# Norm sums of later batches eight steps sooner, k's inverse norms over SyncE's queue, logits further behind the sums: a kernel of channel attention and SwiGLU

## The chip, the cores and the metric

One core of a Trainium2 chip. The metric is the time of one execution in device microseconds (us); lower is better. A run also reports its span (first to last instruction); the time is 1.7 to 1.9 us longer in every run with the row on GpSimd, and 1.9 to 2.6 us longer in every run with it on SyncE, so spans of the two kinds can't be compared as times. Engines: PE (matmuls), PEld (weight loads), DVE (VectorE), ACT (ScalarE), POOL (GpSimd), SP (SyncE, which issues transfers).

## The reference, cut to what matters

```python
B, N, C = (4, 6016, 256)              # q, k, v; then d_ff = 1536
qn = q / (norm(q, axis=1) + 1e-6);  kn = k / (norm(k, axis=1) + 1e-6)
s = kn.transpose(0, 2, 1) @ qn / tau                # 256 x 256 for each batch
a = softmax(s)
x = v @ a
out = (silu(x @ w_gate) * (x @ w_val)) @ w_out      # 24064 x 256
```

The kernel folds `a` into both weights of each batch: `x @ w_gate = v @ (a @ w_gate)`. So a batch needs its softmax before its own large matmuls start, and this preparation is done in the background of the batch before it.

## The kernel before

The loop goes over 48 chunks of 512 (or 384) rows, 12 steps each. Every step has four matmuls for g and v, a silu on ScalarE, a product on VectorE, and two matmuls of the previous chunk's output. In each step a plan of background work may add something for the next batch.

```python
for f in range(FH):                                  # 12 steps of a chunk
    g_ps, v_ps, mv = gv_matmuls(b, ci, f)            # PE, PSUM buffers: 2 for g, 2 for v
    silu = gv_silu(g_ps, mv)                         # ScalarE
    gv_product(f, sv, silu, v_ps, mv)                # VectorE
    prev.step()                                      # PE, output of the previous chunk
    background(b + 1, ci * FH + f)
    # ... v loads (GpSimd's queue), v transposes (SyncE's queue), output copies and stores
```

The background of one batch, in order: loads of q and k, 24 pairs of squares with their sums on GpSimd (`norm_acc`), a split into three bf16 parts, column sums on PE, inverse norms on GpSimd. Those of k lie one to a partition; logits need them along a row. So they go out to DRAM as a row and come back spread over all partitions:

```python
def norm_cols(b):
    # ... column sums on PE, copy on VectorE, two powers on GpSimd -> inv [128, 4]
    row = dram.tile([C], FP32, tag="ink_row")
    nc.gpsimd.dma_start(out=row.rearrange("(h p) -> p h", p=P), in_=inv[:, CH:])
    ink = work.tile([P, C], FP32, tag="ink")
    nc.gpsimd.dma_start(out=ink, in_=row.partition_broadcast(P))

def logits(b, jh):                                   # VectorE waits here for ink
    nc.vector.scalar_tensor_tensor(out=state[b, "s"][:, jh, :], in0=kq[:, jh, :],
        scalar=inv[:, jh:jh + 1], in1=ink, op0=ALU.mult, op1=ALU.mult)
# then: tanh (ScalarE), four reciprocals (VectorE), exponentials (VectorE),
# row sums (PE), twelve weight products (PE)
```

The plan, the same for each later batch (144 steps):

```python
SQ0 = 21;  S1 = SQ0 + (5 * NP) // 2 + 1              # NP = 24, so S1 = 82
plan[S1].append((norm_split,))
plan[S1 + 10].append((norm_cols,))                   # with row and spread in it
plan[S1 + 24].append((logits, 0));  plan[S1 + 25].append((logits, 1))
plan[S1 + 26].append((half_tanh,))
# reciprocals S1+29..32, exponentials S1+33, row sums S1+35, weights from S1+36
```

## Time and profile before

| | |
|---|---|
| median of 3 runs at first, of 4 with the later ones | 812.73 us, 813.04 us (812.66 to 813.95) |
| profiled run | 811.27 us, span 809.5 us |
| PE busy | 98% |
| one step in the steady part | 1.295 us = 6 matmuls, 0.216 us apart |

A line of the page's groups reads: line, engine, operation, tiles, number; busy us, mean ns of one; idle time just before them and what ended it. The prediction shows the lines that matter. The page lists 3,905 PE matmuls and 3,979 weight loads. A second profile of the same kernel (the first experiment) has all the 3,979 matmuls, and its rows of the three large groups end so:

```profile
L439 PE MATMUL g_ps<-vT,Wg 128*128 128x512 bf16 (+1 forms) x1128 | 330.7, 375 | 0.0
L439 PE MATMUL v_ps<-vT,Wv 128*128 128x512 bf16 (+1 forms) x1128 | 330.4, 374 | 0.0
L480 PE MATMUL o_new<-sv,w_out_sb 128*128 128x512 bf16 (+1 forms) x1104 | 324.5, 376 | 0.0
```

The 1.2 to 1.3 us of idle time ahead of each group in the first profile were matmuls without a record, not waits: with all records there the idle time is 0.0.

### The profile page before, as it was taken

The numbers are of one execution on the slowest core, as the hardware profiler recorded it, in microseconds if no ns is written. First come the engines' busy times: TensorE is split into PE (matmuls) and PEld (weight loads), VectorE is DVE, ScalarE is ACT, GpSimd is POOL, SyncE is SP. The second block draws the span as 40 slices with busy tenths as digits, with TensorE's granted clock in tenths as the row PEclk, the third lists the DMA queues.
The fourth block names the chain that finished last, engine by engine and source line by source line (L and its number), as shares of the span: only waits on it lengthen the run. The fifth ranks groups of instructions, "written<-read, shape, count | busy, mean of one in ns | idle before, by whom it ended". The sixth has DMA issues, their size and how long they took to land.

```text
span 809.5 us, 11903 instructions
## 1 busy us (share of the span) xinstructions
PE 790.1 (98%) x3905; PEld 385.5 (48%) x3979; DVE 550.1 (68%) x841; ACT 455.6 (56%) x803; POOL 260.9 (32%) x320
## 2 busy tenths in 40 slices
PE   4999999999999999999999999999999999999998
PEld 2644444444454444444454444444445444444446
DVE  4777887658666778766766787866766665665654
ACT  4566666555555666555555666655555555555553
POOL 4415888431011787722010377742100000000000
PEclk9999999999999999999999999999999999999999
DMA  9995999659798899566889799763866656565533
GB/s 90 144 153 106 146 181 170 127 92 163 126 171 141 173 156 159 151 131 73 162 153 146 157 164 181 128 138 80 185 131 143 137 130 131 144 130 129 117 113 98
DMA packets 201070, 112.34 MB, mean 139 GB/s; under 512 B 149088, under 2 KB 187744, under 8 KB 200256
## 3 DMA queue, kind: packets, MB, share of 16 engines
q1 hardware_dynamic: 182720, 84.11, 44.0%
q0 software_dynamic: 18144, 27.41, 31.6%
q8 instruction: 31, 0.51, 0.3%
q14 instruction: 31, 0.25, 0.1%
q10 hardware_dynamic: 144, 0.07, 0.0%
HBM read 79.04 MB, written 60.43 MB: 172 GB/s over the span
## 4 chain that ended last, share of the span: by engine, by line
PE 95%; DMA 3%; issue 1%; ACT 0%; DVE 0%; POOL 0%; ACTq 0%; POOLq 0%
PE g_ps L439 30%; PE v_ps L439 30%; PE o_new L480 29%; PE ps L408 2%; DMA q_sb<-in_q_dram 2%; PE kq_new L168 2%; PE o_new L533 1%; DMA k_sb<-in_k_dram 1%; ACT silu L445 0%; PE last_ps L557 0%; DVE sv L449 0%; PE ss_new L195 0%; PE kq_new L173 0%; PE ps L398 0%; PE unit_ps L408 0%
## 5 line engine op out<-in xcount | busy, mean ns | idle before, releaser
L449 DVE TENSOR_TENSOR sv<-silu,v_ps 128x512 bf16<-128x512 bf16 (+1 forms) x576 | 387.3, 673 | 224.7 <-ACT silu L445 223.5
L445 ACT ACTIVATE silu<-g_ps 128x512 bf16<-128x512 f32 (+1 forms) x576 | 339.1, 589 | 292.9 <-PE g_ps L439 245.1
L439 PE MATMUL v_ps<-vT,Wv 128*128 128x512 bf16 (+1 forms) x1109 | 326.3, 374 | 1.2
L439 PE MATMUL g_ps<-vT,Wg 128*128 128x512 bf16 (+1 forms) x1105 | 325.8, 375 | 1.3
L480 PE MATMUL o_new<-sv,w_out_sb 128*128 128x512 bf16 (+1 forms) x1078 | 318.9, 375 | 1.2
L439 PEld LDWEIGHTS <-Wv 128*128 128x128 bf16 x1152 | 112.7, 98 | 131.0 <-issue 0.6
L300 POOL TENSOR_TENSOR acc_new<-acc_new,sq 128x512 f32<-128x512 f32 x135 | 156.1, 1156 | 56.0 <-DVE sq L290 41.9
L480 PEld LDWEIGHTS <-w_out_sb 128*128 128x128 bf16 x1104 | 108.0, 98 | 126.3
L439 PEld LDWEIGHTS <-Wg 128*128 128x128 bf16 x1152 | 109.6, 98 | 122.2
L126 POOL DMA_DIRECT2D vb_new<-in_v_dram x47 | 24.2, 516 | 265.5 <-DMA vT<-vb_new 264.6
L490 DVE COPY pl<-o_new 128x512 uint16<-128x512 uint16 (+1 forms) x92 | 62.3, 677 | 9.5 <-ACT pl L489 9.5
L290 DVE TENSOR_TENSOR sq<-q_sb 128x512 bf16<-128x512 fp8e5 x72 | 66.5, 924 | 0.0
L489 ACT COPY pl<-o_new 128x512 uint16<-128x512 uint16 (+1 forms) x92 | 53.2, 578 | 19.3 <-PE o_new L480 17.2
L291 ACT ACTIVATE sq<-k_sb 128x512 bf16<-128x512 fp8e5 x72 | 44.2, 615 | 0.0
L168 PE MATMUL kq_new<-k_sb,q_sb 128*128 128x512 fp8e5 x184 | 35.6, 319 | 0.9 <-DMA q_sb<-in_q_dram 0.9
L111 POOL DMA_DIRECT2D q_sb<-in_q_dram x45 | 25.2, 561 | 14.4 <-DMA k_sb<-in_k_dram 9.9
L168 PEld LDWEIGHTS <-q_sb 128*128 128x256 fp8e5 x184 | 22.9, 140 | 9.4 <-DMA q_sb<-in_q_dram 2.0
L195 PE MATMUL ss_new<-sq,ones_bf 128*128 128x256 bf16 x83 | 14.7, 334 | 11.1 <-ACT sq L185 11.1
L111 POOL DMA_DIRECT2D k_sb<-in_k_dram x42 | 22.9, 549 | 1.2 <-POOLq L741 0.8
L295 POOL TENSOR_TENSOR acc_new<-sq 128x512 f32<-128x512 bf16 x3 | 3.5, 1153 | 49.2 <-DVE sq L290 49.2
L195 PEld LDWEIGHTS <-ones_bf 128*128 128x128 bf16 x83 | 9.3, 117 | 15.1 <-issue 10.9
L408 PEld LDWEIGHTS <-exT 128*128 128x128 bf16 x104 | 10.0, 98 | 10.9 <-DMA w_gate_sb<-in_moe_w_gate_dram 0.2
(98 smaller groups left out, 209.0 us busy)
## 6 DMA issues: line engine op xcount, KB each, us to landing
rows<-pl SPq DMA_DIRECT2D x86, 256.0 KB, 3.1
out_dram<-ot_new SPq DMA_DIRECT2D x43, 512.0 KB, 4.0
vb_new<-in_v_dram POOLq DMA_DIRECT2D x43, 256.0 KB, 4.5
q_sb<-in_q_dram POOLq DMA_DIRECT2D x36, 128.0 KB, 6.4
k_sb<-in_k_dram POOLq DMA_DIRECT2D x33, 128.0 KB, 7.1
ot_new<-rows SPq DMA_TRANSPOSE x92, 3.7
k_sb<-in_k_dram POOLq DMA_DIRECT2D x5, 256.0 KB, 9.0
rows<-pl SPq DMA_DIRECT2D x6, 192.0 KB, 2.4
```

The costliest lines, as they stand in the source:

```text
L111: nc.gpsimd.dma_start(out=dst[:, gs:gs + gm, :], in_=src[b].rearrange("(p s) c -> p s c", s=NS)[:, gs:gs + gm, :])
L168: nc.tensor.matmul(kq[:, jh, :], q_sb[:, ps:ps + 2, js], k_sb[:, ps:ps + 2, :], start=(t == 0 and jh == 0), stop=last, perf_mode=DR, skip_ ...
L290: nc.vector.tensor_mul(sq[:, :pm, 0, :], q_sb[:, ps:ps + pm, :], q_sb[:, ps:ps + pm, :])
L291: nc.scalar.activation(sq[:, :pm, 1, :], k_sb[:, ps:ps + pm, :], ACT.Square)
L300: nc.gpsimd.tensor_tensor(out=acc, in0=acc, in1=sq[:, s, :, :], op=ALU.add)
L408: nc.tensor.matmul(ps, state[b, "exT"][:, jh, ih * P:(ih + 1) * P], (w_gate_sb, w_val_sb)[w][:, jh, cols], start=(jh == 0), stop=(jh == CH ...
L439: nc.tensor.matmul(dst[:, :mv], W[:, kk, fs], vT[:, kk, :mv], start=(kk == 0), stop=(kk == CH - 1))
L445: nc.scalar.activation(silu[:, :mv], g_ps[:, :mv], ACT.Silu)
L449: nc.vector.tensor_mul(sv[:, f, :mv], silu[:, :mv], v_ps[:, :mv])
L480: nc.tensor.matmul(self.o_ps[h][:, :self.mv], w_out_sb[:, f, h * P:(h + 1) * P], self.sv[:, f, :self.mv], start=(f == 0), stop=(f == FH - 1))
L489: nc.scalar.copy(pl[:, 0, :self.mv], halves[:, 0, :self.mv])
L490: nc.vector.tensor_copy(pl[:, 1, :self.mv], halves[:, 1, :self.mv])
```

## The change

Its intent, as far as the code tells: take the round trip of the row out of GpSimd's queue, where the loads behind it stood still, and give the preparation more room ahead of its use. The diff, cut:

```diff
+    def norm_row(b):
         row = dram.tile([C], FP32, tag="ink_row")
-        nc.gpsimd.dma_start(out=row.rearrange("(h p) -> p h", p=P), in_=inv[:, CH:])
+        nc.sync.dma_start(out=row.rearrange("(h p) -> p h", p=P),
+                          in_=state[b, "inv"][:, CH:])
+    def norm_spread(b):
         ink = work.tile([P, C], FP32, tag="ink")
-        nc.gpsimd.dma_start(out=ink, in_=row.partition_broadcast(P))
+        nc.sync.dma_start(out=ink, in_=state[b, "row"].partition_broadcast(P))
@@ plan
-            step = 7 + 11 * (g - half_g)             # half_g = 6; batches 2 and 3
+            step = 9 + 5 * g if b == 1 else 7 + 10 * (g - 7)
-    SQ0 = 21
+        SQ0 = 21 if b == 1 else 13
-    plan[S1 + 10].append((norm_cols,))
-    plan[S1 + 24].append((logits, 0))
+        plan[S1 + 8].append((norm_cols,))
+        plan[S1 + 13].append((norm_row,))
+        plan[S1 + 18].append((norm_spread,))
+        S2 = S1 + (26 if b == 1 else 30)
+        plan[S2].append((logits, 0))
 ...     # tanh, reciprocals, exponentials, row sums, weights follow S2 as they followed S1 + 24
```

From column sums to logits there were 14 steps; now there are 18 in batch 1 and 22 in batches 2 and 3. Logits stand at step 108 in batch 1 and 104 in the others, for 106 before.

More of the change, by code (lines that the diff above doesn't have):

```diff
@@ L331, in norm_cols @@
         state[b, "inv"] = inv
+    def norm_row(b):
         row = dram.tile([C], FP32, tag="ink_row")
-        nc.gpsimd.dma_start(out=row.rearrange("(h p) -> p h", p=P), in_=inv[:, CH:])
+        nc.sync.dma_start(out=row.rearrange("(h p) -> p h", p=P),
+                          in_=state[b, "inv"][:, CH:])
+        state[b, "row"] = row
+    def norm_spread(b):
         ink = work.tile([P, C], FP32, tag="ink")
-        nc.gpsimd.dma_start(out=ink, in_=row.partition_broadcast(P))
+        nc.sync.dma_start(out=ink, in_=state[b, "row"].partition_broadcast(P))
         state[b, "ink"] = ink
@@ L566, in finish @@
                     nc.sync.dma_start(out=self.dst[:, j, cols], in_=last_sb)
-    LOAD0, SQ0 = 9, 21
-    plan = [[] for _ in range(STEPS)]
-    first_loads = [[] for _ in range(STEPS)]
-    early_loads = [[] for _ in range(STEPS)]
-    late_loads = [[] for _ in range(STEPS)]
-    half_g = len(groups) // 2
-    for g in range(len(groups)):
-        for which in range(2):
-            first_loads[LOAD0 + 5 * g].append((load_qk, g, which))
-            step = 7 + 11 * (g - half_g)
-            if step < 0:
-                early_loads[step + STEPS].append((load_qk, g, which))
-            else:
-                late_loads[step].append((load_qk, g, which))
@@ L584 @@
-    for t in range(NP):
-        step = SQ0 + (5 * t) // 2
-        plan[step].append((norm_acc, t))
-        if t % 2 == 1:
-            plan[step + 1].append((gemm1_pair, t - 1))
-            plan[step + 1].append((gemm1_pair, t))
-    S1 = SQ0 + (5 * NP) // 2 + 1
-    plan[S1].append((norm_split,))
-    plan[S1 + 10].append((norm_cols,))
-    plan[S1 + 24].append((logits, 0))
-    plan[S1 + 25].append((logits, 1))
-    plan[S1 + 26].append((half_tanh,))
-    for n in range(4):
-        plan[S1 + 29 + n].append((recip, n))
@@ L598, with make_plan @@
-    plan[S1 + 33].append((exponentials,))
-    plan[S1 + 35].append((row_sums,))
-    for u in range(len(wp_units)):
-        plan[S1 + 36 + (u * 3) // 2].append((wp_unit, u))
+    def make_plan(b):
+        plan = [[] for _ in range(STEPS)]
+        early = [[] for _ in range(STEPS)]
+        for g in range(len(groups)):
+            step = 9 + 5 * g if b == 1 else 7 + 10 * (g - 7)
+            at = plan[step] if step >= 0 else early[step + STEPS]
+            at.append((load_qk, g, 0))
+            at.append((load_qk, g, 1))
+        SQ0 = 21 if b == 1 else 13
+        for t in range(NP):
+            step = SQ0 + (5 * t) // 2
+            plan[step].append((norm_acc, t))
+            if t % 2 == 1:
+                plan[step + 1].append((gemm1_pair, t - 1))
+                plan[step + 1].append((gemm1_pair, t))
+        S1 = SQ0 + (5 * NP) // 2 + 1
+        plan[S1].append((norm_split,))
+        plan[S1 + 8].append((norm_cols,))
[3 more added lines that the diff above has]
+        plan[S2].append((logits, 0))
+        plan[S2 + 1].append((logits, 1))
+        plan[S2 + 2].append((half_tanh,))
+        for n in range(4):
+            plan[S2 + 5 + n].append((recip, n))
+        plan[S2 + 9].append((exponentials,))
+        plan[S2 + 11].append((row_sums,))
+        for u in range(len(wp_units)):
+            plan[S2 + 12 + (u * 3) // 2].append((wp_unit, u))
+        return plan, early
@@ L603, in background @@
+    plans = {b: make_plan(b) for b in range(1, B)}
     def background(b, step):
-        loads = first_loads if b == 1 else late_loads
-        for what, *args in loads[step] + plan[step]:
+        for what, *args in plans[b][0][step]:
             what(b, *args)
         if b + 1 < B:
-            for what, *args in early_loads[step]:
+            for what, *args in plans[b + 1][1][step]:
                 what(b + 1, *args)
```

## The prediction

> **What bounds the kernel now.** I read the page first: the busy shares, the 40 slices, and the chain that ended last.
>
> ```profile
> span 809.5 us, 11903 instructions
> PE 790.1 (98%) x3905; PEld 385.5 (48%) x3979; DVE 550.1 (68%) x841; ACT 455.6 (56%) x803; POOL 260.9 (32%) x320
> PE   4999999999999999999999999999999999999998
> PEclk9999999999999999999999999999999999999999
> PE 95%; DMA 3%; issue 1%; ACT 0%; DVE 0%; POOL 0%; ACTq 0%; POOLq 0%
> ```
>
> PE is 9 tenths or more busy in 38 of 40 slices at the full granted clock; the chain is PE for 95% and a DMA for 3% (the opening loads, 7.1 + 19.1 = 26 us in the chain, which this change leaves alone). But PE's ends are modelled, so "busy" could hide waits. The second reading is therefore the groups of PE with the idle time just before them, the third the spacing of the matmuls.
>
> ```profile
> L439 PE MATMUL v_ps<-vT,Wv 128*128 128x512 bf16 (+1 forms) x1109 | 326.3, 374 | 1.2
> L439 PE MATMUL g_ps<-vT,Wg 128*128 128x512 bf16 (+1 forms) x1105 | 325.8, 375 | 1.3
> L480 PE MATMUL o_new<-sv,w_out_sb 128*128 128x512 bf16 (+1 forms) x1078 | 318.9, 375 | 1.2
> ```
>
> The last number of each row is all the idle time ahead of some 1,100 matmuls: 1.2 + 1.3 + 1.2 = 3.7 us together. The timeline of VectorE gives the beat, since it makes one product per step:
>
> ```profile
> 156.21 0.69 DVE L449 TENSOR_TENSOR sv<-silu,v_ps 128x512 bf16<-128x512 bf16 x1 [0.61 <-ACT silu L445]
> 157.50 0.69 DVE L449 TENSOR_TENSOR sv<-silu,v_ps 128x512 bf16<-128x512 bf16 x1 [0.61 <-ACT silu L445]
> 158.80 0.69 DVE L449 TENSOR_TENSOR sv<-silu,v_ps 128x512 bf16<-128x512 bf16 x1 [0.61 <-ACT silu L445]
> ```
>
> One step is 1.295 us. It has six 512-column matmuls (two for g, two for v, two of the output product), which start 0.216 us apart in the trace: 6 x 0.216 = 1.296 us. So a step is PE's issue rate and nothing else. I summed the whole loop the same way, from the intervals between matmul starts: g and v 44 full chunks x 48 x 0.216 = 456.2 and 4 short ones x 48 x 0.1625 = 31.2; output product 43 x 24 x 0.216 + 3 x 24 x 0.1625 = 234.6; k'q of three later batches 36 groups x 0.446 = 16.1; weight products 72 x 0.216 = 15.6 and some 3.5 of the first batch's; sums of columns 48 x 0.025 = 1.2; last two chunks 9.1. That is 767.5 us. From the first g matmul (about 39 us) to the end of the last matmul at 806.25 us there are about 767. The only irregular gaps that I find in matmul starts between 45 and 790 us are three of 0.067 us (at 194.3, 388.0 and 581.7), one per later batch.
>
> **What the skill says.** "TensorE: Matmul & The Clock Gate", section "Wait — 56ns, not 53.3ns?", gives back-to-back 512-column matmuls as 215.7 ns start to start once warm. The trace agrees (215 to 216 ns), so no spacing is left to win. "DMA: Bandwidth & Descriptors", section "SWDGE vs HWDGE vs iDMA", says that SyncE's path has descriptors made by hardware and sets up faster than GpSimd's. The trace has the row only on GpSimd's path (0.82 us issue, 8.9 to 9.6 to landing); what SyncE will take is open. The same page, "Issuing engines are not separate DMA queues", says that both run on the same 16 DMA engines, so moving the row does not take its small packets away. The same page, "Two DMAs through the same engine are not ordered", says the reader must wait on the writer's semaphore; the built program has that wait (the spread waits for the row on SyncE), so one queue does not make the pair free.
>
> **The change part by part.** No matmul, activation, product or copy is added or removed: the order of the built programs shows 7,950 PE rows in both and the same kinds elsewhere. Six small DMA issues (3 rows, 3 spreads) move from GpSimd to SyncE. The rest is placement. Step numbers are of a batch's 144 steps.
>
> 1. *Row on SyncE.* Takes off GpSimd: its stand-still between the two issues,
>
> ```profile
> POOL ink L336 <- DMA row<-inv: 26.1, 3, 9.1
> DVE s_new L344 <- DMA ink<-row: 0.6, 1, 0.6
> 166.32 0.82 POOL L334 DMA_DIRECT2D row<-inv  x1 [0.29 <-POOL inv L330]
> 175.48 0.58 POOL L336 DMA_DIRECT2D ink<-row  x1 [8.34 <-DMA row<-inv]
> ```
>
> 26.1 us in three waits, and 3 x (0.82 + 0.58) = 4.2 us of issues. None of it is on the path: GpSimd is 32% busy. What it does is hold back the q, k and v loads behind it: four q and k issues and one v load stand at 176 to 178 us right after the spread. They will go out at about 165. Gain on PE: 0.
>
> 2. *Wait at logits.* VectorE stood 0.6 us for the spread in one batch (second line above). With logits 2 steps later (batch 1: 108 for 106) and the spread about 5 steps ahead that goes. But PE had no gap there, since two PSUM buffers per product absorb it. Gain: 0.
>
> 3. *Eight steps sooner.* Batches 2 and 3 run the 24 squares and sums at steps 13 to 70 for 21 to 78, the split at 74 and the column sums at 82. The same work in a shifted place: a step with a square costs VectorE 0.6 + 0.86 = 1.46 us against 1.295, a step with a copy too 2.06; squares meet copies (step 5 or 11 of a chunk) four times per batch before and after. Column sums come 8 steps after the split for 10. In the trace the split ends at 150.8 us and PE reads it at 162.5: 11.7 us of room, about 9 left. Gain 0, loss 0.
>
> 4. *Reciprocals and exponentials.* This is where the three 0.067 us come from, as far as I can see: four 0.94 us reciprocals (0.86 start to start) put VectorE 4 x 0.165 = 0.66 us behind, a copy in the middle 0.6 more, in all 1.26. Batch 1 keeps a copy among them (step 113), batches 2 and 3 (steps 109 to 112) do not. Expected: two of three gaps go, 0.13 us.
>
> 5. *Loads.* q and k groups of batches 2 and 3 come every 10 steps for 11, seven of twelve in the batch before for six. PE uses each group at least 21 steps (27 us) after its issue (last: step 47 against 68); landing is 6 to 10 us. The same bytes.
>
> Sum: 812.73 - 0.13 = **812.6 us**. The most that could ever be won is the 3.7 us of PE idle, 0.46%.
>
> **The rivals.** *Rival A: v starves.* The transposed v of a chunk passes through GpSimd (load), SyncE (transpose) and then PE, and SyncE works in order. In the trace the shortest room is here:
>
> ```profile
> 253.20 1.23 SPq L504 DMA_TRANSPOSE ot_new<-rows  x1
> 254.53 1.25 SPq L135 DMA_TRANSPOSE vT<-vb_new  x1
> ```
>
> The chunk it serves starts at 261.5 us: 7.0 us, of which 3.7 are landing, leaves 3.3; in quiet stretches issue to use is 25.9. The room shrinks from 22 us at 160 to 7 at 254 because each spill of planes takes up to 10 us beside q/k loads, and because the row goes with a hole of 7 to 8 us in all DMA traffic (no packets from about 170 to 177). If the denser loads cost 4 us more, PE would wait a few us per batch: 815 to 820. Against it: the hole no longer holds GpSimd, so v loads start about 12 us earlier, and the row comes 8 steps sooner for batches 2 and 3, further from this stretch. I give it 10% of any visible wait and 1% of over 2%.
>
> *Rival B: the spread arrives late.* The row waits on SyncE for GpSimd's inverse, the spread for the row. Batch 1: inverse at about 163.4 us, row issued about 166 (after the transpose at step 94), landed at 175 if it takes 9 us as before, spread landed 6 us later at 181; logits at step 108 are at 181.7 + 2 x 1.3 = 184.3. Room 3 us, more if hardware descriptors are quicker; batches 2 and 3 have 4 steps more. Were it 5 us late, VectorE would stop and PE with it about 1 us after: 815 at worst for three batches.
>
> *Rival C: the freed GpSimd makes something faster.* It is 26 us of idle time that nobody on PE waited for; only room grows. Speaks for no gain beyond item 4.
>
> **Range and chances.** The three runs of before span 812.66 to 813.35; the profiled one took 811.27. I take 811.8 to 814.0: below, hardly more than the spread between runs, because PE has nothing to give; above, a wait of 1 us under A or B. Faster by over 2% would need 16 us out of 3.7 us of idle, which cannot be: 0.003. Slower by over 2% needs rival A in all three batches: 0.012. Same: 0.985.
>
> **What would show it.** Right: the three PE idle numbers stay near 1.2; step beat 1.295; PE 98%; the wait of GpSimd for the row gone from the list of waits, and the wait of VectorE for the spread too; 0.067 us gaps in batch 1 alone; v transposes of the chunks after the row issued with at least 7 us of room. GpSimd's long waits for a v buffer grow by about what the row wait loses. Wrong: PE idle of over 0.5 us before a g matmul at a chunk's start (rival A), or VectorE waiting before the logits with a PE gap after (rival B), or SyncE's row taking far over 9 us.

## The result, and the profile after

Ratios in this document are the mean time of one kernel's runs over that of the other's in the same rounds, so they are not quite the ratio of the medians.

| | before | after |
|---|---|---|
| median, 4 runs each | 813.04 us (812.66 to 813.95) | 811.69 us (810.87 to 812.56) |
| ratio | | 0.9982 (0.9965 to 0.9999) |
| span of the profiled run | 809.5 us | 809.0 us |

The time is the same by the 2% measure and 0.2% lower in fact: 1.35 us between the medians, where 0.13 us were predicted, and 811.69 is 0.1 us under the range. The page after, head and PE's large groups:

```profile
span 809.0 us, 11969 instructions
PE 793.5 (98%) x3979; PEld 385.0 (48%) x3979; DVE 550.3 (68%) x841; ACT 454.7 (56%) x803; POOL 256.7 (32%) x314
...
L445 PE MATMUL g_ps<-vT,Wg 128*128 128x512 bf16 (+1 forms) x1128 | 330.7, 375 | 0.0
L445 PE MATMUL v_ps<-vT,Wv 128*128 128x512 bf16 (+1 forms) x1128 | 330.3, 374 | 0.0
L486 PE MATMUL o_new<-sv,w_out_sb 128*128 128x512 bf16 (+1 forms) x1104 | 324.6, 376 | 0.0
```

PE is as full as before. The spans of the two profiles are 0.51 us apart, and that divides exactly. From the first silu to the last it is 761.38 us before and 761.25 after: 0.13 us, two of the three gaps of 0.067 us gone (one is left, at 196.9 us in batch 1). From the end of the last matmul to the end of the span it is 3.25 us before and 2.85 after: 0.40 us. But the metric is the time, and by that the profiled run of before took 811.27 us and that of after 811.54, 0.27 longer. So the 1.35 us between the medians are not in these two executions.

The queues did change. From the list of waits after (who waited for what: us in all, times, longest), the lines of GpSimd:

```profile
POOL vb_new L126 <- DMA vT<-vb_new: 256.7, 19, 18.2
...
POOL den L359 <- ACT th L358: 73.1, 3, 27.6
```

the line of SyncE's queue for the row:

```profile
SPq L342 <- DMA row<-inv: 14.1, 2, 10.8
```

and SyncE's timeline (start us, duration, what) in batch 1:

```profile
164.60 0.58 SPq L336 DMA_DIRECT2D row<-inv  x1
168.46 0.35 SPq L501 DMA_DIRECT2D rows<-pl  x1
179.58 0.33 SPq L342 DMA_DIRECT2D ink<-row  x1
180.62 1.25 SPq L510 DMA_TRANSPOSE ot_new<-rows  x1
```

GpSimd no longer waits for the row; SyncE does, and holds the output's transposes behind it. The three rows took 15.0, 15.0 and 11.1 us from issue to landing, for 8.9, 9.6 and 9.1 before on GpSimd's queue. The packet records tell the two apart: before, the first row went as 16 packets of 64 bytes, all between 167.75 and 167.94 us, and was reported landed 7.2 us later; after, as 256 of 4 bytes, nearly all between 167.85 and 173.55 us. So the spread of batch 1 landed at 183.2 us, 1.3 us ahead of its use at 184.5; in batches 2 and 3 it was 3.1 and 9.2 us ahead. In the two profiles of the kernel before, these rooms are 0.1 to 0.8 us:

| room between landing of k's spread and logits, us | batch 1 | batch 2 | batch 3 |
|---|---|---|---|
| before, first profile | 0.2 | 0.1, after 0.56 of waiting | 0.8 |
| before, second profile | 0.6 | 0.1 | 0.7 |
| after, first profile | 1.3 | 3.1 | 9.2 |
| after, second profile | 2.1 | 3.6 | 9.5 |

That gave the theory that the experiments test. **The edge:** the kernel before needs the spread at just the moment when it lands. The profiled executions had it in time; executions with slower DMA have not, and PE loses a microsecond or two. **Rivals:** it is noise of the runs alone; or it is the queue; or the spread loads; or the earlier sums. One more has no experiment: the part before the loop, whose length differs by over a microsecond between executions (next section).

### The profile page after: what moved, and what is told of

Same layout as the page of the kernel before. It is cut to its first block, busy times and chain, and to the rows that moved or that the text cites. A ratio compares the mean times of both kernels' runs of the same rounds, so it can differ in the third digit from the quotient of the medians.

```text
span 809.0 us, 11969 instructions
## 1 busy us (share of the span) xinstructions
PE 793.5 (98%) x3979; PEld 385.0 (48%) x3979; DVE 550.3 (68%) x841; ACT 454.7 (56%) x803; POOL 256.7 (32%) x314
## 3 DMA queue, kind: packets, MB, share of 16 engines
q1 hardware_dynamic: 183968, 84.51, 44.8%
q0 software_dynamic: 17904, 27.01, 31.6%
## 4 chain that ended last, share of the span: by engine, by line
PE 96%; DMA 3%; issue 0%; DVE 0%; POOL 0%; POOLq 0%
PE g_ps L445 30%; PE v_ps L445 30%; PE o_new L486 29%; PE ps L414 2%; DMA q_sb<-in_q_dram 2%; PE kq_new L168 2%; PE o_new L539 1%; DMA k_sb<-in_k_dram 1%; PE ps L404 0%; PE last_ps L563 0%; PE ss_new L195 0%; PE kq_new L173 0%; PE unit_ps L414 0%; PE cs L324 0%; POOL k_sb L111 0%
## 5 line engine op out<-in xcount | busy, mean ns | idle before, releaser
L445 PE MATMUL g_ps<-vT,Wg 128*128 128x512 bf16 (+1 forms) x1128 | 330.7, 375 | 0.0
L445 PE MATMUL v_ps<-vT,Wv 128*128 128x512 bf16 (+1 forms) x1128 | 330.3, 374 | 0.0
L486 PE MATMUL o_new<-sv,w_out_sb 128*128 128x512 bf16 (+1 forms) x1104 | 324.6, 376 | 0.0
L126 POOL DMA_DIRECT2D vb_new<-in_v_dram x47 | 24.2, 514 | 257.6 <-DMA vT<-vb_new 256.7
L168 PEld LDWEIGHTS <-q_sb 128*128 128x256 fp8e5 x184 | 22.1, 136 | 10.2 <-DMA q_sb<-in_q_dram 2.8
L359 POOL TENSOR_SCALAR den<-th 128x512 f32<-128x512 f32 x3 | 1.8, 615 | 73.1 <-ACT th L358 73.1
```

The costliest lines, as they stand in the source:

```text
L168: nc.tensor.matmul(kq[:, jh, :], q_sb[:, ps:ps + 2, js], k_sb[:, ps:ps + 2, :], start=(t == 0 and jh == 0), stop=last, perf_mode=DR, skip_ ...
L445: nc.tensor.matmul(dst[:, :mv], W[:, kk, fs], vT[:, kk, :mv], start=(kk == 0), stop=(kk == CH - 1))
L486: nc.tensor.matmul(self.o_ps[h][:, :self.mv], w_out_sb[:, f, h * P:(h + 1) * P], self.sv[:, f, :self.mv], start=(f == 0), stop=(f == FH - 1))
```

## The experiments

All ratios are to the kernel before in the same rounds; the first four ran on one chip, the second four on another.

### The kernel before against itself

No edit but a comment.

> The kernel before, unchanged but for a comment. Both theories: the ratio to itself shows what 5 rounds can tell apart. Theory A (the 1.35 us between the medians is mostly run-to-run: clock windows and launch): ratio within 0.9985 to 1.0015, single runs spread over 1.5 us or more, and the time of a run follows its granted clock. Theory B (a real wait of over 1 us was removed): runs spread under 0.7 us.

Measured: 812.15 us (811.35 to 812.80), ratio 0.9989 (0.9978 to 1.0001). One program differs from itself by 0.1%, with an interval that just holds 1. Single spans go from 809.6 to 811.0 here and from 810.1 to 812.8 in the 11 other runs of it, and don't follow the granted clock: 810.1 came with 0.995, 810.9 with 1.000. So the guess that the clock explains the spread fell. Theory B's spread of under 0.7 us fell too (1.45 us in time here, 2.71 in the other 11). And a difference under some 0.1% can't be told in five rounds. Something else moves this program by up to 3 us. The opening is part of it: in the ten profiles the first silu of the loop starts between 39.8 and 41.1 us: in six of them by 40.2, in four from 40.9 on.

### The changed kernel again

No edit but a comment.

> The changed kernel once more. Theory A: 0.0 to 0.7 us faster than before (0.13 us is real), ratio 0.999 to 1.0005. Theory B: again 1.0 to 1.7 us faster, ratio 0.9979 to 0.9988.

Measured: 811.17 us (810.88 to 811.93), ratio 0.9981 (0.9968 to 0.9994). The gain repeats, at the size that a real wait was said to have. Against the copy of the kernel before in the same rounds it is smaller: 0.76 us between the means (811.27 for 812.04). The spans go from 808.8 to 810.0 only.

### The plan alone

```diff
-        plan[S1 + 13].append((norm_row,))
-        plan[S1 + 18].append((norm_spread,))
+        # in norm_cols again: nc.gpsimd.dma_start(row), nc.gpsimd.dma_start(ink)
```

> The changed plan of steps, with the row and its spread left on GpSimd's queue. Theory A: same as before and as the change, within 0.5 us; two of the three 0.067 us gaps gone. Theory B: it gains either all of the 1.35 us (the plan did it) or none (the queue did it).

Measured: 811.17 us (811.01 to 812.26), ratio 0.9984 (0.9972 to 0.9995); room at logits 4.7, 10.0 and 8.9 us. Most of the gain comes with the plan and without SyncE's queue: the median is that of the change, 811.17 us, and the means are 0.28 us apart (811.55 for 811.27). One finding speaks for the queue, though: in this profile a transpose of v was issued 4.3 us before its chunk began, with 3.4 us to land. Over the ten profiles this least room, counted after the first row, is 4.3 to 10.0 us in the six with the row on GpSimd, the kernel before among them, and about 10.7 to 17.9 in the four with it on SyncE. PE waited for v in none of them.

### The queue alone

```diff
     plan[S1 + 10].append((norm_cols,))
+    plan[S1 + 13].append((norm_row,))                # SyncE
+    plan[S1 + 18].append((norm_spread,))             # SyncE; logits stay at S1 + 24
```

> The kernel before with only the row and the spread moved to SyncE's queue (steps 95 and 100), logits left at step 106. The trace of the change had the row 15 us from issue to landing and 3.6 us more for the spread, so the spread lands at about 185 us and VectorE waits some 3 us at logits of batch 1 (at 181.7); PE loses 1 to 2 us in batch 1 and perhaps as much in the others: 1 to 6 us slower than before. If instead the queue was the gain (theory B), it is 1 us faster.

Measured: 820.1 us (817.31 to 823.19), ratio 1.0087 (1.0068 to 1.0107): 7 us slower, a little over the 1 to 6 expected. From the list of waits:

```profile
DVE s_new L349 <- DMA ink<-row: 7.0, 3, 4.5
```

and PE's timeline in batch 2:

```profile
379.80 0.59 PE L444 MATMUL g_ps<-vT,Wg 128*128 128x512 bf16 x2
383.47 1.01 PE L444 MATMUL v_ps<-vT,Wv 128*128 128x512 bf16 x2 [3.07 <-DVE sv L454]
384.28 1.06 PE L485 MATMUL o_new<-sv,w_out_sb 128*128 128x512 bf16 x2
```

Two matmuls that start at 379.80 should be followed 0.43 us later; it took 3.67, a gap of 3.24 us. VectorE had stood 4.47 us for the spread. The gap has a second cost: two matmuls take 1.01 and 1.06 us behind it, for 0.59. From 383.47 to 386.80 us the granted clock is 0.52, most matmuls start 0.427 us apart for 0.216, and another 1.56 us are lost. The loop as a whole is 6.2 us longer than in the first profile of before: 1.12 and 0.30 in batch 1 (0.30 while VectorE catches up), 3.24 and 1.56 in batch 2. The queue by itself is a loss, and all of it arises at logits.

### Logits three steps later, and nothing else

```diff
-    plan[S1 + 24].append((logits, 0))
+    plan[S1 + 27].append((logits, 0))
 ...  # all that follows, 3 steps later too; row, queue, loads and sums as before
```

> The kernel before with logits and all after it 3 steps (3.9 us) later; row, loads and sums untouched. Edge theory (before stands at the edge: k's spread landed 0.1 to 0.8 us ahead of logits in both traces of it, so in executions with slower DMA PE waits): spread 4 us ahead of logits in the trace, none of the three 0.067 us gaps, spans of single runs fall to 809.2 to 810.4 as those of the change, ratio to before 0.9978 to 0.9990. Rival (the queue, the loads or the earlier sums give the gain): 0.999 to 1.0005.

Measured: 811.15 us (810.96 to 812.78), ratio 0.9982 (0.9970 to 0.9993); room at logits 3.7, 2.5 and 3.5 us; no irregular gap at all in PE from 45 to 790 us. The room in batches 2 and 3 is less than the 4 us expected, and two spans (810.3, the profiled one, and 811.0) stand apart from the other four (809.2 to 809.4). The profiled one had its first silu at 41.06 us, 1.0 later than in the first profile of before, and its loop took 761.19 us for 761.38: so its higher span is all opening. The gain of the whole change, from one number in the plan. The rival that the queue, the loads or the sums are needed for it falls.

### Logits two steps earlier

```diff
-    plan[S1 + 24].append((logits, 0))
+    plan[S1 + 22].append((logits, 0))
```

> The kernel before with logits and all after it 2 steps (2.6 us) earlier. Edge theory: VectorE waits some 2 to 2.6 us at logits in each of the three batches, of which PE's buffers take about 1.2: 3 to 6 us slower than before. Rival (the room at logits doesn't matter, buffers take it): within 0.5 us of before.

Measured: 820.34 us (817.41 to 823.06), ratio 1.0088 (1.0068 to 1.0108). More than expected, because the landing was late as well and because of the clock:

```profile
DVE s_new L344 <- DMA ink<-row: 10.0, 3, 4.1
```

The waits in the three batches were 3.70, 4.15 and 2.16 us, and the gaps between PE's matmuls at these places 2.47, 2.91 and 0.93: each time 1.23 to 1.24 us less. The two waits of the queue alone that cost PE something lie on the same line (2.36 us gave a gap of 1.12, and 4.47 one of 3.24). So 1.23 us of a wait at logits cost PE nothing, as I read it because the PSUM buffers bridge them, and PE pays what is over it. After the longest gap it pays more: behind the 2.91 us the granted clock is 0.53 from 382.0 to 385.5 us, as behind the 3.24 us above, and 1.68 us more are lost; behind 2.47 us and less the matmuls keep their 0.216 us. With that the sum closes: 2.47 + 2.91 + 0.93 + 1.68, less the three gaps of 0.067 that this plan lacks, is 7.79 us, and the loop took 769.17 us for 761.38.

### The loads alone

```diff
-            step = 7 + 11 * (g - half_g)
+            step = 7 + 10 * (g - 7)
```

> The kernel before with the changed plan of q and k loads alone (every 10 steps, seven in the batch before). Edge theory: same as before within 0.7 us, ratio 0.9990 to 1.001, since room at logits stays 0.1 to 0.8 us. Rival (spreading the loads gives the gain): 0.9978 to 0.9988. Rival A of the prediction (v starves): slower by over 1 us.

Measured: 812.66 us (812.07 to 813.00), ratio 0.9996 (0.9984 to 1.0008). The loads give nothing. But its profile (span 811.2 us) caught what the profiles of before did not. VectorE, and then PE, at logits of batch 2:

```profile
375.71 0.69 DVE L449 TENSOR_TENSOR sv<-silu,v_ps 128x512 bf16<-128x512 bf16 x1 [0.60 <-ACT silu L445]
378.19 0.48 DVE L344 SCALAR_TENSOR_TENSOR s_new<-kq_new,inv,ink 128x256 f32<-128x256 f32 x1 [1.79 <-DMA ink<-row]
378.59 0.68 DVE L449 TENSOR_TENSOR sv<-silu,v_ps 128x512 bf16<-128x512 bf16 x1
```

```profile
378.34 0.59 PE L439 MATMUL g_ps<-vT,Wg 128*128 128x512 bf16 x2
379.32 0.59 PE L439 MATMUL v_ps<-vT,Wv 128*128 128x512 bf16 x2 [0.39 <-DVE sv L449]
379.75 0.59 PE L480 MATMUL o_new<-sv,w_out_sb 128*128 128x512 bf16 x2
380.18 0.59 PE L439 MATMUL g_ps<-vT,Wg 128*128 128x512 bf16 x2
380.91 0.59 PE L439 MATMUL v_ps<-vT,Wv 128*128 128x512 bf16 x2
```

The spread landed 1.79 us after VectorE was free for it. Starts of PE should be 0.43 us apart; 378.34 to 379.32 is 0.98, a gap of 0.55 us, which is the wait less 1.24 again; 380.18 to 380.91 is 0.73, another 0.30 while VectorE catches up. In all 0.85 us are lost. The same batch in the first profile of the kernel before waited 0.56 us, under the 1.23 that cost nothing, and PE lost nothing. That is the edge, seen in one execution, of a kernel with other loads.

### The row as two packets

The changed kernel, with k's inverse norms turned by PE first, so that the row leaves as 2 runs of 512 bytes and not as 256 of 4 bytes.

```diff
+        tr = psum_m.tile([CH, P], FP32, tag="misc")
+        nc.tensor.transpose(tr, state[b, "inv"][:, CH:], identf)
+        row_sb = work.tile([CH, P], FP32, tag="row_sb")
+        nc.vector.tensor_copy(row_sb, tr)
-        nc.sync.dma_start(out=row.rearrange("(h p) -> p h", p=P), in_=state[b, "inv"][:, CH:])
+        nc.sync.dma_start(out=row.rearrange("(h p) -> h p", p=P), in_=row_sb)
```

> The changed kernel with k's inverse norms turned into two rows by a transpose on PE, so that the row goes out as 2 packets of 512 bytes and not as 256 of 4 bytes. If the small packets make the 11 to 15 us to landing and the hole in DMA traffic: landing in 2 to 4 us, room at logits over 8 us in batch 1. If the queue or traffic makes it: landing stays over 8 us. Time: as the change within 0.5 us, since PE doesn't wait there (1 transpose a batch, some 0.1 us each, is added).

Measured: 811.54 us (811.39 to 812.31), ratio 0.9986 (0.9974 to 0.9998), no better and no worse than the change that can be told. SyncE's timeline of batch 1:

```profile
167.96 0.31 SPq L340 DMA_DIRECT2D row<-row_sb  x1
168.62 0.36 SPq L504 DMA_DIRECT2D rows<-pl  x1
172.16 0.33 SPq L345 DMA_DIRECT2D ink<-row  x1
175.61 1.23 SPq L513 DMA_TRANSPOSE ot_new<-rows  x1
```

The spread waits for the row, and goes out 4.2 us after it, where the change needed 15.0; in batches 2 and 3 it is 6.9 and 3.8 us. Room at logits is 8.3, 10.2 and 14.2 us, over the 8 expected in batch 1. So on SyncE's queue the form of the transfer, and not the queue or the traffic, makes most of the time of the row. (On GpSimd's queue, with packets of 64 bytes, it takes 8.3 to 11.5 us.) The two packets are not worth it here: the loop from first to last silu takes 761.58 us for 761.25, and PE did not wait at logits any more.

### The tail

From the end of the last matmul to the end of the span: 3.24 or 3.25 us in the six profiles with the row on GpSimd (before twice, plan alone, logits later and earlier, loads alone), and 2.83 to 2.85 us in the four with it on SyncE (the change twice, queue alone, row as two packets). The difference lies after the last store has landed (1.30 or 1.31 us to the end, against 0.93 or 0.94): SyncE then passes seven semaphore waits 0.06 us apart in the first six, a single one in the other four. I read it as a matter of where the last store stands in the order of these waits, which shifts with the number of transfers on the queue. The records fit: SyncE has 281 transfers in the first six and 287 in the other four, and the last store's semaphore is the second of eight in that order there and the eighth here, six places on. That is argued, not shown.

Most of the tail's 0.40 us is no gain in time. The time is 1.79 us longer than the span in the mean of the runs with the row on GpSimd, and 1.99 to 2.20 in the means of the four sets of runs with it on SyncE, so 0.2 to 0.4 us come back outside the span.

## Why the prediction was wrong

**Right.** PE's issue rate sets the time and the change takes no work from it: step 1.295 us, 98% busy. (The full traces have 7,958 PE rows in both kernels, not 7,950.) Two of the three 0.067 us gaps went, and only batch 1 kept one; the waits of GpSimd for the row and of VectorE for the spread are gone from the list. The loads and the earlier sums are worth nothing (0.9996 for the loads; the sums were not run by themselves, but logits alone give the whole gain). v did not starve: the least room after the row is 13.1 us in the first profile and about 10.7 in the second, over the 7 asked for. "Same" holds.

**The step that failed** is item 2, the wait at logits: "But PE had no gap there, since two PSUM buffers per product absorb it. Gain: 0." The trace had the sign: VectorE waited 0.56 us in batch 2, and the rooms in the others were 0.2 and 0.8 us. I read one execution, in which the wait stayed under the 1.23 us that cost nothing, as if every execution were so. Room that is about nil in all three batches means that slower landings go over that line. The times of the kernel before vary from 811.27 to 814.57 us, and those of the change from 810.87 to 812.56; logits alone give 0.9982. Of the mean difference in time to the change in the same rounds (812.82 against 811.27: 1.55 us), 0.13 are the gaps and about 0.1 the tail; about 1.3 us is the rest.

That the gain comes when logits stand later is shown by moving them alone: mean time 811.55 for 812.95, 1.40 us less, of which three gaps are 0.2. That the other 1.2 us are PE waiting at logits is inferred. For it speak the losses when the room is taken away (7 us with logits two steps earlier), the one execution of the kernel with other loads, and the spans: the first profile of before, in which PE did not wait there, took 809.5 us, and none of its 22 runs beside the experiments came under 810.1 (its copy had two of five at 809.6 and 809.7), while four of six runs with later logits lie at 809.2 to 809.4. Three things stay open. No profile fell on such an execution of the kernel before itself. The opening differs by 1.2 us between profiles, as much as the gain; its code is the same in both kernels, but no run shows how often it is long in each. And the kernel before differed from its own copy by 0.78 us in mean time (812.82 against 812.04), so the 1.3 us are uncertain by most of a microsecond; against the copy, 0.5 us would be the rest.

**The range** failed with it: "below, hardly more than the spread between runs, because PE has nothing to give". The 3.7 us of idle time that I took as a ceiling were missing records, and what PE gave was, as far as can be inferred, in executions that no profile showed. The tail was in no step of the sum either, but it is about 0.1 us of time. By how much the range was missed is partly chance: the median lies 0.11 us under it, less than the 0.78 us between one program and its copy; the repeat, at 811.17, lies 0.63 under it.

**Rival B** was closer to the truth than its working. "landed at 175 if it takes 9 us as before": it took 15.0 us, which I had named as a sign of being wrong, so the 3 us of room were 1.3. "DMA: Bandwidth & Descriptors", section "SWDGE vs HWDGE vs iDMA", calls the hardware path faster to set up. The issue itself agrees (0.43 to 0.58 us for the row in the change, 0.81 to 0.83 on GpSimd), but the landing does not follow it: 11.1 to 15.0 us against 8.3 to 11.5. The change bore it only because it moved logits too; with the queue alone it cost 7 us, for the 2 us or so that I gave the rival at worst. The same page's "Issuing engines are not separate DMA queues" is not contradicted: the packets only changed queue (by part 3 of the two pages, GpSimd's queue went from 18,144 to 17,904 packets and SyncE's from 182,720 to 183,968) and became more. Which DMA engines took them no run here shows.

**Rival C**, that the freed GpSimd gives no time of its own, holds. My detail of it was wrong: its waits for a v buffer did not grow (264.6 to 256.7 us, 263.2 in the second profile of the change); the free time shows as waiting for the tanh (18.2 to 73.1 us).

**Rival A**, v starving, did not come. (The shortest room in the first trace was 6.8 us, at 448.59, not the 7.0 that I showed.) So the queue needs the plan: later logits bear SyncE's slow row. The plan does not need the queue as far as the time shows; what SyncE's queue adds is room for v, 13.1 us for the 4.3 of the plan alone, which no run here put to use.

## What to carry to other kernels

When a wait on a transfer is about as long as its room in one profile, treat it as a cost of some executions, not as zero: look at the room in all the places where it is needed, and compare the spans of all runs, not the profiled one. Before moving work to another queue, move its consumer later by itself; here that one number gave the gain and the queue alone lost 7 us. A gap of PE can also cost more than its length: here 1.6 to 1.7 us more behind the two of 2.9 us and over. And count the records of a group before taking a small idle time for a ceiling.

## What the Trainium skill lacked or had wrong

- "DMA: Bandwidth & Descriptors", "SWDGE vs HWDGE vs iDMA": calls hardware descriptors faster to set up and does not say what that is worth in landing; for 1 KB in 4-byte runs from SBUF to DRAM the runs show 11.1 to 15.0 us on SyncE's queue in the changed kernel (10.0 to 14.4 with the queue alone) and 8.3 to 11.5 on GpSimd's.
- The same page, "Why small descriptors are slow (HBM only)", treats packets of 256 bytes or so and has no figure for 4 bytes: as 2 runs of 512 bytes the row was done within 3.8 to 6.9 us, for 11.1 to 15.0 as 256 of 4 bytes.
- "Perfetto Trace Analysis", "Tensor Engine Instruction (MATMUL, LD_WEIGHTS)", says that the ends of matmuls are estimated, not that records can be missing: 3,905 of 3,979 in one profile made 3.7 us of idle time that a full one has at 0.0.
- No page found says that the end of a program can depend on how many transfers a queue has had: 3.24 or 2.84 us from the last matmul to the end of the span, with six transfers moved from one queue to another.
